# One pool of eight PSUM banks, the last batch's outputs in halves, and a new written order for a fused attention and gated-convolution kernel

## The chip, the cores and the metric

The kernel runs on one core of a Trainium2 chip. A core has TensorE (PE), which multiplies matrices and writes only to PSUM; VectorE (DVE) and ScalarE (ACT), which both read and write PSUM and on-chip memory; GpSimd (POOL); and SyncE (SP), which in this kernel only issues DMA transfers. The engines run side by side, each works through its own instructions in the order in which they are written, and semaphores make one wait for another. PEld in the profile is TensorE's weight load, which overlaps its matmuls.

The metric is the device time of one execution in microseconds (us). Three runs of the kernel before gave 364.24, 364.77 and 365.52 us, a median of 364.77 us.

## The reference

Eight batches `b`, eight heads, 512 tokens, 32 state tokens, head width 64. First each batch goes through a two-way attention between its tokens `x` and its state tokens; both results lie one behind the other, so that a batch then has 544 rows of 512 values. Those rows go through a gated layer of width 1024 with a three-tap convolution along the rows:

```python
scores = scale * x @ state.T            # softmax over 32 state tokens, then @ state   -> xread
scores2 = scale * state @ x.T           # softmax over 512 tokens,      then @ x       -> sread
x = concatenate([xread, sread], axis=2) # heads side by side: (8, 544, 512)
h = maximum(x @ w_in, 0)                # 512 -> 1024
conv = conv_w[0]*h[s-1] + conv_w[1]*h[s] + conv_w[2]*h[s+1]
out = (h * sigmoid(conv)) @ w_out       # 1024 -> 512
```

## The kernel before, in words

**Tiling.** The width of 1024 is cut into eight slices `f` of 128; a step `i = 8 b + f` is one slice of one batch, 64 steps in all. The 512 tokens of a batch are four chunks `c` of 128 rows. The heads are handled in two groups `g` of four.

**One step.** For a batch other than the first, TensorE does six matmuls of 128x128 by 128x512 into a bank `ps_h` (`hidden`, L593): attention weights `a` and the state-times-w_in matrix `u` are each split in a high and a low part of a 32-bit type that TensorE takes in one pass (fp32r), and three of the four products are kept. ScalarE or VectorE takes the bank out as `h` (`relu`, L194 or L196); `middle` (L188 or L190), two taps on VectorE (L619, L624), tanh (L628), `gate` (L633) and a split in high and low (L199, L202) follow. Then `project` (L651) does three matmuls for each of the four chunks into four banks `acc`, which are open over the eight steps of a batch. When they are full, `end` takes each out (L665 on ScalarE, L667 on VectorE) and `store` (L685) sends it off from SP. The first batch goes without the split, in plain fp32 (L588 and L659).

**Beside the steps** stand, for each batch, the scores (`scores`, L300), the transposes of the state tokens' softmax (`flip`, L328), the read of `x` with them (`read`, L341, which needs the transfer `xx`), a small transpose (`read_flip`, L352), and the products of state and w_in (`state_product`, L508, two for each batch but the first; `block_product`, L527, for the first). For the state tokens of four batches at a time there are `state_hidden` (L574) and `tail` (the `acc_t` rows of L651); `tail_store` (L722) sends a lot's rows off in four DMAs. The weights come in through a rounding on ScalarE and VectorE (L237 to L254). In the profile's shapes "128*128", "64*32" and "128*32" say what part of TensorE's array a matmul uses: L651, L593, L588, L574, L328 and L352 use 128*128, L300, L508 and L527 64*32, L341 and L461 128*32.

**Buffers.** PSUM has eight banks. Before, three pools share them: four `acc` (also the first batch's scores and flips), two `ph` (hidden products and the filler), two `ps` (everything else). The transfers `xt` have four buffers, `xx` has one, so that a batch's `xx` can be loaded only when the `read` of the one before is done.

**Order.** Nothing is scheduled when the kernel is built. All work is added as numbered operations with what they read and write, and a written table of these numbers, `ORDER`, says in which order they are issued; a `v` behind a number puts an operation on VectorE that else is on ScalarE, and a negative number puts that many idle matmuls (L209) on TensorE. The words such as "act" or "keep2" that `add` takes, and `IN_TURN`, are not read when the kernel is built. The order of the transfers on SP comes from the same table.

```python
            i = int(word.rstrip("v"))
            if i < 0:
                fns += [self.fill] * -i
                continue
            assert after[i] <= done and i not in done, "an operation before one that it needs"
            fns.append(partial(self.ops[i][2], on=self.vector) if word[-1] == "v" else self.ops[i][2])
```

Of the kernel before, what the change touches and what calls it, by code (L numbers as in the profile page):

```python
# [16 lines left out]
B, H, S, NS, D = 8, 8, 512, 32, 64  # L17
# [10 lines left out]
NL = 4  # L28
# [21 lines left out]
PSUM = dict(acc=4, ph=2, ps=2)  # L50
# [4 lines left out]
121 120 0 98 -10 123 100 99 101 102 103 124v 2 -6 141 4 3 126 5 14 125 -3 149 8 142 15 143 6 17 127 16 7 144 9 -1 444  # L55
# [3 lines left out]
527v 245 455 454 199 495 53 76 512 507 528 513 515v 526 502 514 508 75 516 77 517 160 161 162 52 54 496 550 62 551 201  # L59
# [7 lines left out]
1632 365 366 628 573 602 629 643 615 616 630 119 1633 574 603 617v 632 1634 220 367 644 645 646 587 618 588 647 1635  # L67
# [3 lines left out]
677 693 726 624 328 407 678 679 694 653 332 664 408 234 680 707v 681 665 666 641 656 676 640 237 695 238 696 657 756  # L71
235 333 682 409 708 335 655 757 758 691 709 683 236 741 639 261 593 595 323 654 727 710 667 668 728 730 760 697 410
291 330 670 685 771 414 711 415 712 336 759 729 706 772 773 775 731 331v 337 334 329 405 338 742 743 774 416 411 262
672 669 263 713 776 368 761 684 417 671 745 418 686 698 264 412 699 816 762 413v 374 339 763 764 340 732 765 341 419
420 421 687 714 265 422 718 266 766 746 423 701 777 747 376 700 702 377 369 733 375 267 778 734 717 301 371 372 292
735 748 779 786 715 720 1496 780 719 817v 818 364 721 311 312 787 1497 314 286 736 749 820v 716 315 831 750 801 788
744 781 802v 370 724 313 751 737 268 832 287 833 378 379 722 380 834 269 803 819 804 302 790v 791 789 740 738 270 755
723 271 273 739 792 274 272 835 805 754 282 752 793 794 821 806 836 837 795 767 796 822 753 769 294 770 381 884 382
807 885 886 838 839 303 768 854 869 887 823 808 783 785 855 809 288 784 840 856 824 293 857 304 899 782 810 888 295
799 797 800 275 1498 825 305 858v 900 859 811 889 841 890 815 901 306 860 903 904 870v 278 902 279 871 873 812 798 814  # L80
905 906 1499 289 826 290 1500 861 907 908 276 862 813 827 307 296 1501 297 277 842 829 844 929 828 843 830 1502 845
872 1504 874 308 875 1505 1506 891 424 930 944 1507 914 309 298 1508 892 1509 1510 876 931 425 1512 945 426 846 299
300 863 915 310 909 916 917 847 959 933 1513 864 478 479 918v 484 1514 427 485 1515 482 483 848 934 480 935 849 725
# [3 lines left out]
385 1536 984 1029 1013 1014 1016v 1537 1538 911 913 997 1535 924 966 1539 1540 1541 1017 986 1542 967 895 910 1543 486  # L87
# [3 lines left out]
1007 974 352 1042 346 1043v 979 1020 975 1044 1021 353 1045 995 1059 1030 1072 996 994 1060 1009 1011 1046 1061 355  # L91
347 348 1033 1087 391 1062 356 1022 1034 1088 1063 1047 1035 980 1010 1026 1024 1036 1025 1073 993 1008 1023 1048 1037
349 1064 1039 1038 1040 1049 1074 1075 1089 1091 354 350 1076v 351 1041 393 1092 1050 1093 1051 1052 1077 1155 394
1156 395 1065 1090 1110 1054 1157 1094 1140 1055 396 1078 1079 1111 1066 1080 1159v 1160 1125 1095 1096 1081 1141 1126
1562 1067 1158 1112 1127 1053 1113 1056 1071 397 1082 1068 357 1083 1069 1070 360 358 1128 1142 1097 1161 1129v 1114
1084 361 359 1115 1162 1170 1163 1116 1144 1086 1171 1098 1130 1117 1131 1145 1118 1132 981 1099 1104 1164 1215 1085
1133 392 1134 1119 1146 1216v 1165 1147 1200 1100 1201v 1105 1101 1202 1217 1102 1103 1219 1253 1218 1172 1185 1120
1108 1174 1143 1220 1135 432 1221 1109 1148 1204 1205 1563 1106 1149 1206 1150 1175 1207 1186 1121 1208 1203 1136 1122
1123 1107 1124 1137 439 1152 1167 440 1138 1139 1222 1153 1187 1189v 1254v 1255 1256 1188 1190 1173 1191 1192 1257v
1209 1223 1176 1258 1177 1238 1193 1151 1268 1154 1239v 442 441 1178 1259 1283 1194 1179 1169 1269v 1284 443 1240 1270  # L100
1180 1168 1285 1183 1286 1184 398 1272 1195 399 401 1287v 1210 1288 1166 1289 402 1199 1182 1198 1197 1224 1181 1260
1242 1290 1273 400 1243 1274 1244 1196 1291 1275 1261 1211 1343 1213 1214 1328 1225 1245 1246 1226 1212 1276 1227 1232
1344v 1262 1229 1329v 1241 1330 1313 1247 1298 1263 1332 1248 1299 1333 1251 1345 1300 1228 1271 1301 434 1233 1292
1346 1234 1236 1235 1250 1252 1267 433 1334 1335 437 1302v 1293 1303 1277 435 1331 1314 1315 438 1317 1278 1347v 1230
1231 1237 436 1265 1266 1280 1366 1249 1304 1305 1306 1307 1367 1264 1368 1282 1396 1336 1318 1319 1320 1370v 1279
1348 1294 1371 1349 1337 1281 1297 1295 1372 1426 1338 1308 1397 1350 1310 1351 1321 1322 1381 1398 1373 1369 1316
1400v 1564 1565 1296 1401 1323 1566 1567 1427 1568 1570 1402 1571 1374 1428 1399 1430v 1431 1382v 1383 1311 1326 1384
1572 1385v 1386 1312 1341 1309 1411 1325 1375 1324 1340 1327 1342 1387 1573 1352 1403 1404 1412 1432 1353 1413 1569
1356 1415v 1574 1388 1471 1414 1575 1576 1416 1433 1577 1578 1417 1355 1441 1579 1580 1581 1360 1418 1376 1361 1339
1357 1389 1582 1472v 1473 1583 1474 1584 1475v 1362 1390 1442 1443 1363 1354 1380 1476 1391 1378 1429 1586 1405 1587  # L110
1406 1588 1393 1408 1395 1456 1585 1410 1589 1358 1434 1419 1590 1591 1445v 1446 1592 1594 1595 1457 1359 1364 1596
# [45 lines left out]
def fused_kernel(ctx: ExitStack, tc: tile.TileContext, xT, xn, stT, w_in, conv_w, w_out, out):  # L157
# [49 lines left out]
    def fill():  # L207
        idle.append(bank("idle", "ph")) if not idle else None
        PE.matmul(idle[0][:, :P], ident, ident, start=True, stop=True)  # L209
# [684 lines left out]
```

## Time and profile before

| what | us |
|---|---|
| median of three runs | 364.77 |
| the profiled execution: its time | 364.56 |
| the profiled execution: its span, first to last instruction | 362.8 |
| busy in the span: PE / PEld / DVE / ACT / POOL | 356.2 / 264.7 / 325.0 / 244.8 / 58.8 |

The page's busy times are shares of the span. A matmul's row runs from its start to the modelled end of its pipeline, so that rows of neighbours overlap, and a TensorE that reads as busy may still wait between two starts. The chain of waits, which follows the last instruction back through what released it, shows the net piece of each group of matmuls instead; from such pieces one sees how long a group holds TensorE. VectorE's and ScalarE's rows overlap by a little too. Times in a view are in us from the start of the span unless marked ns, and "x24" says how many instructions a row groups. Transfers run on 16 DMA engines; the windows' last two columns give their busy share and the GB/s moved.

### The profile page before, as it was taken

To read this page: it belongs to the slowest core of one execution; us is meant where nothing else is said; L and a number is where in the kernel's file an instruction comes from. 1 tells how busy PE (TensorE), PEld (TensorE's weight loads), DVE (VectorE), ACT (ScalarE), POOL (GpSimd) and SP (SyncE) were. 2 spreads that over 40 slices of the span, in tenths; PEclk is the share of its full clock that TensorE was granted. 3 is DMA by queue.
4 is the path that set the end of the run, shared out by engine and by line. 5 is a ranking of instruction groups with operands and counts; after the bars stand their busy time and mean duration, and the time that the engine had idled before them with its cause. 6 is when DMAs were issued, how large, how long until landed. Compare 5 with 4: busy or idle time off the path is not lost.

```text
span 362.8 us, 6645 instructions
## 1 busy us (share of the span) xinstructions
PE 356.2 (98%) x2498; PEld 264.7 (73%) x2498; DVE 325.0 (90%) x577; ACT 244.8 (67%) x494; POOL 58.8 (16%) x159
## 2 busy tenths in 40 slices
PE   7999999999999999999999999999999999999995
PEld 6753557676668876878898877877877778888884
DVE  2999999999999999999999999988989968988761
ACT  2999998885868777565857665845764457445731
POOL 1014103130201112130101201111312212111000
PEclk9999999999999999999999999999999999999999
DMA  7999784033240342200020012000200002002004
GB/s 247 399 357 394 285 327 142 2 117 116 78 157 0 117 146 75 101 4 0 31 87 0 2 58 89 30 0 3 82 33 2 0 29 89 1 0 89 30 2 144
DMA packets 12384, 35.05 MB, mean 97 GB/s; under 512 B 1472, under 2 KB 2880, under 8 KB 11328
## 3 DMA queue, kind: packets, MB, share of 16 engines
q1 hardware_dynamic: 12352, 34.63, 26.2%
q8 instruction: 19, 0.31, 0.3%
q14 instruction: 13, 0.11, 0.1%
HBM read 25.71 MB, written 8.91 MB: 95 GB/s over the span
## 4 chain that ended last, share of the span: by engine, by line
PE 89%; ACT 4%; DVE 3%; DMA 1%; issue 1%; SPq 0%; DVEq 0%
PE acc L651 45%; PE ps_h L593 21%; PE ps_u L508 4%; PE ps_h L588 4%; PE acc_t L651 3%; PE ps_s L300 2%; PE ps_hs L574 2%; PE acc_c L651 2%; PE ps_r L341 1%; DMA st<-stT 1%; PE ps_t L328 1%; PE ps_s L461 1%; PE idle L209 1%; ACT e L319 1%; ACT hc L237 1%
## 5 line engine op out<-in xcount | busy, mean ns | idle before, releaser
L651 PE MATMUL acc<-wo,g 128*128 128x512 f32 x708 | 175.8, 394 | 0.1
L651 PEld LDWEIGHTS acc<-wo,g 128*128 128x128 f32 x708 | 130.8, 188 | 36.8 <-issue 5.0
L593 PE MATMUL ps_h<-a,u 128*128 128x512 f32 x336 | 84.9, 393 | 0.0
L593 PEld LDWEIGHTS ps_h<-a,u 128*128 128x128 f32 x336 | 62.3, 188 | 18.0 <-issue 2.5
L199 ACT ACTIVATE g<-t 128x512 fp32r<-128x512 f32 (+1 forms) x60 | 36.9, 621 | 21.2 <-DVE t L633 14.0
L619 DVE SCALAR_TENSOR_TENSOR t<-h,cw,t 128x511 f32<-128x511 f32 x64 | 47.4, 746 | 1.8 <-ACT t L188 1.5
L608 POOL COPY hs<-h 128x1 f32<-128x1 f32 x64 | 27.0, 436 | 132.5 <-ACT h L194 109.9
L624 DVE SCALAR_TENSOR_TENSOR t<-h,cw,t 128x512 f32<-128x512 f32 (+1 forms) x64 | 47.1, 745 | 1.4
L603 POOL COPY h<-hs 128x1 f32<-128x1 f32 x56 | 25.3, 458 | 136.0 <-DVE t L633 127.9
L628 ACT ACTIVATE t<-t 128x512 f32<-128x512 f32 x64 | 39.6, 627 | 11.0 <-DVE t L624 10.7
L202 DVE TENSOR_TENSOR g<-t,g 128x512 fp32r<-128x512 f32 (+1 forms) x60 | 40.2, 676 | 3.7 <-ACT g L199 3.4
L633 DVE SCALAR_TENSOR_TENSOR t<-t,h 128x512 f32<-128x512 f32 (+1 forms) x64 | 41.8, 663 | 1.6 <-ACT t L628 1.4
L194 ACT ACTIVATE h<-ps_h 128x512 f32<-128x512 f32 x51 | 30.1, 595 | 14.1 <-PE ps_h L593 11.1
L188 ACT ACTIVATE t<-h,cw 128x512 f32<-128x512 f32 x40 | 28.3, 720 | 1.3 <-DVE h L196 1.0
L665 ACT ACTIVATE o<-acc 128x512 f32<-128x512 f32 (+1 forms) x30 | 17.3, 584 | 12.9 <-PE acc L651 12.6
L199 ACT ACTIVATE u<-ps_u 128x512 fp32r<-128x512 f32 x28 | 16.1, 595 | 10.4 <-PE ps_u L508 10.4
L202 DVE TENSOR_TENSOR u<-ps_u,u 128x512 fp32r<-128x512 f32 x28 | 18.7, 681 | 2.8 <-ACT u L199 2.8
L574 PEld LDWEIGHTS ps_hs<-sr,wi 128*128 128x128 f32 x128 | 14.9, 192 | 1.1 <-ACT sr L356 0.4
L508 PE MATMUL ps_u<-wi,st 64*32 64x512 f32 x224 | 15.2, 601 | 0.0
L588 PE MATMUL ps_h<-p,u 128*128 128x512 f32 x32 | 15.2, 608 | 0.0
L574 PE MATMUL ps_hs<-sr,wi 128*128 128x128 f32 x128 | 15.2, 276 | 0.0
L240 ACT ACTIVATE raw<-raw 128x512 uint32<-128x512 uint32 (+1 forms) x17 | 11.2, 669 | 5.8 <-DMA raw<-conv_w 4.8
(95 smaller groups left out, 409.9 us busy)
## 6 DMA issues: line engine op xcount, KB each, us to landing
xt<-xT SPq DMA_DIRECT2D x16, 512.0 KB, 6.3
xx<-xn SPq DMA_DIRECT2D x8, 1024.0 KB, 5.1
out<-o SPq DMA_DIRECT2D x30, 256.0 KB, 2.1
raw<-w_in SPq DMA_DIRECT2D x8, 512.0 KB, 6.9
raw<-w_out SPq DMA_DIRECT2D x8, 512.0 KB, 9.0
out<-o_t SPq DMA_DIRECT2D x8, 64.0 KB, 1.7
st<-stT SPq DMA_DIRECT2D x1, 448.0 KB, 5.5
out<-o_c SPq DMA_DIRECT2D x1, 256.0 KB, 2.8
```

What stands on the lines that cost most here:

```text
L194: A.activation(dst, src, AF.Relu, scale=0.5)
L199: A.activation(hi, src, AF.Copy)
L202: engine.tensor_tensor(lo, src, hi.bitcast(F32), op=ALU.subtract)
L508: PE.matmul(ps_u[b, hf, g][j * NS:(j + 1) * NS, :], st[half, b * NP + j, :], wi[half, j, hf * 512:(hf + 1) * 512], start=True, stop=True)
L574: PE.matmul(ps_hs[m, f][:, :NT], wi[:, k, f * P:(f + 1) * P], sr[m][:, k, :], start=(k == 0), stop=(k == NK - 1))
L588: PE.matmul(ps_h[i], u[0][:, g, fs], pa[0][:, g, :], start=(g == 0), stop=(g == NG - 1))
L593: PE.matmul(ps_h[i], u[j][:, g, fs], a[k][:, g, :], start=(n == 0), stop=(n == 3 * NG - 1))
L619: V.scalar_tensor_tensor(t[:, 1:], h[:, :S - 1], cw[:, f, 0:1], t[:, 1:], op0=ALU.mult, op1=ALU.add)
L624: V.scalar_tensor_tensor(t[:, :n], h[:, 1:n + 1], cw[:, f, 2:3], t[:, :n], op0=ALU.mult, op1=ALU.add)
L628: A.activation(tt[i], tt[i], AF.Tanh, scale=0.25)
L633: V.scalar_tensor_tensor(tt[i][:, :n], tt[i][:, :n], 1.0, hd[i][:, :n], op0=ALU.add, op1=ALU.mult)
L651: PE.matmul(acc, g[j][:, cs], wo[:, k, f, :], start=(f == 0 and n == 0), stop=(f == NF - 1 and n == 2))
```

## The change

Five things are different.

1. **One pool.** The pools `acc=4`, `ph=2`, `ps=2` become one pool `ps=8`. Every bank is asked for from it, so that an `acc`, a hidden product or a transpose may take any free bank, and the tags by which operations wait for each other become ("ps", ...).
2. **The last batch's outputs.** Batch 7 was stored in whole chunks of 128x512, only its last chunk in two halves of 128x256; now all four chunks are evacuated and stored in halves. Their buffers come from `xt`, `xt`, `e2` and `o`. An `end` can now be put on ScalarE or on VectorE by the table.
3. **Stores of state tokens.** The four DMAs of a lot's state tokens were one operation; each is now an operation that the table can place by itself.
4. **The table.** `ORDER` is written anew as a whole: the numbers of later operations are shifted by the added ones, the filler goes from 23 matmuls to 18, and the v-marks are others. By the built order 9 `middle`, 3 `relu` and the 2 `e2t` copies go from VectorE to ScalarE, one copy of `u` goes the other way, and six of the output evacuations are on VectorE (3 whole, 3 halves), before two. Beyond the filler, no matmul is added or dropped.
5. **Names of kinds** (`mid2`, `vk2`, `store1`), which the built kernel doesn't read.

```diff
-PSUM = dict(acc=4, ph=2, ps=2)
+PSUM = dict(ps=8)
...
 ORDER = """
-121 120 0 98 -10 123 100 99 101 102 103 124v 2 -6 141 4 3 126 5 14 125 -3 149 8 142 15 143 6 17 127 16 7 144 9 -1 444
...
-1491
+120 121 0 98 -10 123 99 100 101 102 8 103 9 124v -6 141 2 11 10 125 3 149 126 142 12 -1 143 150 151 13 127 14 4 15 131
...
+1497 1488 1486 1487 1489 1470 1485 1498 1500 1499 1501
...
-            ps_s[NG * b + g] = bank(f"ps_s_{b}_{g}", "ps" if b else "acc")
+            ps_s[NG * b + g] = bank(f"ps_s_{b}_{g}")
...
-        ps_h[i] = bank(f"ps_h_{i}", "ph")
+        ps_h[i] = bank(f"ps_h_{i}")
...
-            accs[b, c] = bank(f"acc_{b}_{c}", "acc")
+            accs[b, c] = bank(f"acc_{b}_{c}")
...
     def parts_of(b, c):
-        n = 2 if (b, c) == (B - 1, NCH - 1) else 1
+        n = 2 if b == B - 1 else 1
...
-    def out_tag(b, c):
-        return "o" if b < B - 1 else "xt" if c < NCH - 1 else "e2"
-
-    def end(b, c, q, engine):
+    def out_tag(b, c, q):
+        return "o" if b < B - 1 else ("xt", "xt", "e2", "o")[c]
+
+    def end(b, c, q, on=A):
...
-    def tail_store(m):
-        o = outs["t", m]
-        for i in range(NL):
-            nc.sync.dma_start(out[NL * m + i, S:, :], o[i * NS:(i + 1) * NS, :])
+    def tail_store(m, i):
+        nc.sync.dma_start(out[NL * m + i, S:, :], outs["t", m][i * NS:(i + 1) * NS, :])
...
-                    on = b == B - 1 and (c + q) % 2
-                    cost = ("tt3" if on else "keep2") if parts > 1 else "tt" if on else "act"
-                    o = (out_tag(b, c), "o", b, c, q)
-                    add("DVE" if on else "ACT", cost, partial(end, b, c, q, V if on else A),
-                        r=[("acc", b, c)], w=[o])
+                    o = (out_tag(b, c, q), "o", b, c, q)
+                    add("ACT", "keep2" if parts > 1 else "act", partial(end, b, c, q), r=[("ps", "acc", b, c)], w=[o],
+                        other="vk2" if parts > 1 else "tt")
...
-            add("SP", "store", partial(tail_store, m), r=[("o", "t", m)])
+            for i in range(NL):
+                add("SP", "store1", partial(tail_store, m, i), r=[("o", "t", m)])
```

What the new table moves, at the three places of which the prediction speaks. In these rows the name left of the arrow is the tile written, those right of it are read, and the last number of a name counts buffers.

TensorE, in the middle of the program, before: the product of state and w_in of batch 4 (`ps_u`, eight matmuls of 32x512) stands alone between a hidden product or projections of full width.

```order
L593 MATMUL ps_h_1768<-a_2_1363,u_2_1_1409 128x512
L651 MATMUL acc_1_1339<-wo,g_15_1540 128x512
L651 MATMUL acc_1_1339<-wo,g_15_1539 128x512 x2
L508 MATMUL ps_u_0_0_1794<-wi,st 32x512
L508 MATMUL ps_u_0_1_1795<-wi,st 32x512
...
L651 MATMUL acc_2_1314<-wo,g_15_1540 128x512
L651 MATMUL acc_2_1314<-wo,g_15_1539 128x512 x2
```

The change, the same product: the read of `xx` of another batch (`ps_r`, 32 matmuls) now stands directly ahead of it.

```order
L651 MATMUL acc_1_1374<-wo,g_14_1609 128x512
L651 MATMUL acc_1_1374<-wo,g_14_1608 128x512 x2
L341 MATMUL ps_r_1679<-xx_1638,e2t_1673 32x64 x16
L341 MATMUL ps_r_1679<-xx_1638,e2t_1629 32x64 x16
L508 MATMUL ps_u_0_0_1716<-wi,st 32x512
L508 MATMUL ps_u_0_1_1717<-wi,st 32x512
...
L651 MATMUL acc_3_1344<-wo,g_14_1609 128x512
L651 MATMUL acc_3_1344<-wo,g_14_1608 128x512 x2
```

Before, TensorE left the full-width matmuls twice for these two pieces of work; now it leaves them once.

SP, the first transfers, before: the `xx` of the first batch stands behind the seventh block of weights (`raw`).

```order
L233 DMA raw_257<-w_in 128x2x512
L233 DMA raw_319<-w_in 128x1024
L233 DMA raw_326<-w_in 128x1024
L233 DMA raw_335<-w_in 128x1024
L292 DMA xx_373<-xn 128x2048
L233 DMA raw_420<-w_in 128x1024
L836 DMA st<-stT 128x896
```

The change: the rest of the state (`st`), five `xt` and six weights stand ahead of it.

```order
L233 DMA raw_241<-w_in 128x2x512
L833 DMA st<-stT 128x896
...
L288 DMA xt_433<-xT 128x1024
L288 DMA xt_435<-xT 128x1024
L233 DMA raw_439<-w_out 128x1024
L288 DMA xt_493<-xT 128x1024
L292 DMA xx_495<-xn 128x2048
```

The `xx` of the first batch went from the twelfth transfer of the program to the twenty-first.

SP, the last stores, before: the four stores of state tokens stand between the last two stores of outputs.

```order
L685 DMA out<-o_3_1_3945 128x256
L685 DMA out<-o_3_0_3958 128x256
L685 DMA out<-o_0_0_3953 128x512
L685 DMA out<-o_1_0_3955 128x512
L722 DMA out<-o_t_3975 32x512 x4
L685 DMA out<-o_2_0_3987 128x512
```

The change: they stand ahead of the eight halves of the last batch, and the last store is a half.

```order
L720 DMA out<-o_t_3936 32x512 x4
L685 DMA out<-o_2_0_3955 128x256
L685 DMA out<-o_1_1_3969 128x256
...
L685 DMA out<-o_0_1_3976 128x256
L685 DMA out<-o_3_0_3988 128x256
L685 DMA out<-o_3_1_3990 128x256
```

Between the last store of state tokens and the program's last store stand seven halves now; before nothing stood between them.

More of the change, by code (lines that the diff above doesn't have):

```diff
@@ L71 @@
[L71 to L80, printed above, removed]
@@ L92 @@
[L92 to L101, printed above, removed]
@@ L102 @@
[L102 to L106, printed above, removed]
@@ new lines @@
+144 -1 145 20 5 17 129 6 21 22 132 146 147 16 23 7 444 18 447 148 1 44 32 46 33 240 239 24 19 152 134 153 25 130 135
+45 445 154 35 47 48 450 451 446v 26 155 448 34 449 156 38 27 242 49 29 28 30 243 245 128 31 40 452 39 244 41 36 42 37
[13 rows of a table added]
+625 664 640 690 228 238 678 661 665 652 235 666 236 627 692v 706 334 676 667 642 233 286 653 668 337 368 404 403 406
[4 rows of a table added]
+765 314 816 421 751 370 315 779 263 372 808 377 788 287 340 715 831 832 264 766 790v 833 809 774 265 737 791 266 722
+292 724 341 817 780 818 378 375 820v 792 267 270 740 271 819 755 804 789 273 793 835 725 268 723 289 752 738 753 770
@@ new lines @@
+272 739 290 294 754 295 769 794 269 720 781 274 784 869 422 301 854 767 302 721 288 810 870 379 768 783 782 899 282
+834 380 795 871 873 855 884 856 836 821 303 1503 822 796 823 304 858v 874 857 824 305 825 811 423 885 886 1504 837 296
[9 rows of a table added]
+973 1013 1548 1014 1550 1016 1043 974 985 975 1044 390 1541 1551 988 1087 1046 976v 1003 1552 989 1553 1004 342 1554
+980 981 1047 1017 990 1005 1018 1555 991 957 992 1556 1006 972 1072 1549 1019 1073 1020 1015 1074 1048 1021 1057 1558
+1058 393 352 1559 343 1022 978 1007 1560 344 486 1036 487 1076 1088 996 1557 1561 1077 1049 1562 1050 391 1037 979
@@ new lines @@
+1563 355 345 993 1059 1089 1045 1060 1090 1011 1026 1008 1023 995 1041 1564 356 346 994 1010 1091v 347 353 348 394
+1051 1025 1078 349 1052 350 1009 1038 1024 1565 1039 354 1040 351 1054 1055 395 1140 1566 1061 1079 1080 396 397 1092
+1062 1567 1063 1064 1141 392 1155 1569 977 1093 1065 1570 1156v 1571 1094 1053 1110 1125 1066 1142 1075 1568 1143 1095
+1067 1126 1081 1157 1144 1111v 1112 1127 1129 1082 1145 1146 1130 1238 1056 357 1069 1159 358 1128 1070 1147 1084 1085
+1071 360 1114v 1148 1131 1115 1283 1068 359 361 1116 1117 1132 1096 1133 1097 1160 1185 1083 1186 1086 1200 1100 1149
@@ new lines @@
+1101 1161 1170 1158 1187 1188 1113 1098 1150 1201 1162 1134 1215 1099 1163 1189 1118 1190 1135 1119 1106 1108v 1120
+1171v 1124 1216 1109 1107 1164 1172 1174v 1122 1104 1175 1165 1137 398 1139 1105 432 1123 1176 1177 401 399 1178 1102
+1103 1202 1173 1217 402 1204v 1219 1138 1205 1220 1218 1239v 1206 1153 1152 1121 1136 1168 1151 1240 1166 1268 400
+1191 1242 1241 1298 1253 1179 1180 1192 1193 1243 1221 1194 1222 1195 1244 1223 1245 1299 1246 1269v 1154 1169 1184
+1199 1183 1270 1271 1167 1207 1272v 433 1208 1209 1181 1196 434 1210 1254 1273 1255 1203 1300 1224 1284 1285 1256 1286
@@ new lines @@
+1225 1572 1257v 1182 1197 1343 1212 1274 1258 1287 435 437 1275 1211 1227 438 436 1276 1247 1248 1302v 1313 1214 1198
+1314 1232 1213 1303 1228 1288 1328 1315 1289 1290 1291 1304 1259 1260 1234 1235 1277 1366 1261 1344v 1278 1317 1305
+1262 1233 1329v 1345 1301 1346 1330 1306 1263 1318 1251 1332 1229 439 1226 1333 440 1250 442 1367 1292 443 1249 1266
+1265 1252 1267 1293 1264 1279 1280 1319 1334 1335 1347 1320 1336 1368 1370v 1282 1369 1371 1316 1348 1573 1281 1294
+1381 1574 1307 1236 1321 1372 1575 1349 1373 1322 1230 1382v 1576 1396 1297 441 1374 1577 1441 1411 1350 1397v 1308
@@ new lines @@
+1337 1579 1295 1296 1398 1351 1442 1399 1331 1383 1443 1426 1323 1400v 1445v 1471 1311 1326 1310 1401 1338 1309 1312
+1385 1402 1327 1580 1578 1386 1403 1444 1324 1384 1581 1342 1404 1582 1583 1231 1237 1352 1584 1585 1325 1387 1388
+1587 1472v 1389 1588 1412 1589 1353 1413 1473 1590 1591 1592 1446 1427 1428 1447 1430 1448 1390 1340 1355 1341 1456
+1586 1474 1414 1593 1431 1595 1357 1596 1597 1391 1598 1375 1376 1599 1449 1378 1339 1600 1601 1429 1415 1475 1457
+1458 1416 1417 1432 1611 1364 1418 1405 1379 1356 1594 1612 1602 1380 1394 1354 1365 1476 1406 1613 1614 1459 1460v
@@ L207, in fill @@
     def fill():
-        idle.append(bank("idle", "ph")) if not idle else None
+        idle.append(bank("idle")) if not idle else None
         PE.matmul(idle[0][:, :P], ident, ident, start=True, stop=True)
@@ L364, in attention @@
         add("PE", "scores", partial(scores, b), r=[("st", int(b > 0)), ("xt", NG * b), ("xt", NG * b + 1)],
-            w=[("at", b)] + [("ps", "s", b, g) if b else ("acc", "s", g) for g in range(NG)])
+            w=[("at", b)] + [("ps", "s", b, g) if b else ("ps", "acc", "s", g) for g in range(NG)])
         for g in range(NG):
-            add("ACT", "act", partial(keep_scores, NG * b + g), r=[("ps", "s", b, g) if b else ("acc", "s", g)] + [("at", b)] * g,
+            add("ACT", "act", partial(keep_scores, NG * b + g), r=[("ps", "s", b, g) if b else ("ps", "acc", "s", g)] + [("at", b)] * g,
                 w=[("scores", b, g)] if g else [("at", b), ("scores", b, g)], other="tt")
@@ L448, in first_flip @@
     def first_flip(g):
-        ps_x[g] = bank(f"ps_x_{g}", "acc")
+        ps_x[g] = bank(f"ps_x_{g}")
         for c in range(NCH):
@@ L487, in first_softmax @@
     def first_softmax(g):
-        x, s, m, n, p = ("acc", "x", g), ("acc", "s", g), ("s1", "m0", g), ("s1", "s0", g), ("pa", g)
+        x, s, m, n, p = ("ps", "acc", "x", g), ("ps", "acc", "s", g), ("s1", "m0", g), ("s1", "s0", g), ("pa", g)
         add("PE", "flip", partial(first_flip, g), r=[("scores", 0, g), ("at", 0)], w=[x])
@@ L779, in step @@
             r += [(x, b, f // 4, q) for x in ("uhi", "ulo") for q in range(NG)]
-        add("PE", "hidden" if b else "hidden0", partial(hidden, i), r=r, w=[("ph", i)])
-        add("ACT", "act", partial(relu, i), r=[("ph", i)], w=[h], other="tt")
+        add("PE", "hidden" if b else "hidden0", partial(hidden, i), r=r, w=[("ps", "h", i)])
+        add("ACT", "act", partial(relu, i), r=[("ps", "h", i)], w=[h], other="tt")
         if b:
@@ L784, in step @@
         add("POOL", "pool", partial(edge, i), r=[h], w=[("edge", i)] + ([("corner", f)] if b == 0 else []))
-        add("ACT", "middle", partial(middle, i), r=[h, ("weight", W_CONV)], w=[t], other="two")
+        add("ACT", "middle", partial(middle, i), r=[h, ("weight", W_CONV)], w=[t], other="mid2")
         add("DVE", "tap", partial(before, i), r=[h], w=[t])
@@ L799, in step @@
                 r=[*g, ("weight", W_OUT + f) if i >= WHOLE else (f"g{f % 2}", "w", f)],
-                w=[("acc", b, c)])
+                w=[("ps", "acc", b, c)])
         if f == NF - 1:
```

20 lines of the change are left out of this document (6 added, 14 removed), and 49 rows, old and new, of the table ORDER.

## The prediction

> **What bounds the kernel now.** I read four views: the page's busy shares, the windows, the groups of TensorE by shape, and the chain of waits in order of time. The busy shares first, and four windows of the first half (columns: engine busy us with instruction counts for PE, PEld, DVE, ACT, POOL; granted clock; DMA share; GB/s).
>
> ```profile
> span 362.8 us, 6645 instructions
> ...
> PE 356.2 (98%) x2498; PEld 264.7 (73%) x2498; DVE 325.0 (90%) x577; ACT 244.8 (67%) x494; POOL 58.8 (16%) x159
> ```
>
> ```profile
> 0.00:10.00 10.00, 7.89 (x56) 6.79 (x57) 2.78 (x8) 3.48 (x7) 1.73 (x23) 1.00 0.81 260
> 10.00:20.00 10.00, 9.94 (x193) 7.60 (x195) 9.50 (x23) 9.42 (x22) 0.00 (x0) 1.00 1.01 389
> 20.00:30.00 10.00, 10.00 (x140) 4.33 (x132) 9.93 (x20) 8.80 (x18) 3.42 (x3) 1.00 1.01 371
> 30.00:40.00 10.00, 10.00 (x60) 3.68 (x53) 9.96 (x19) 9.77 (x20) 2.47 (x8) 1.00 1.01 401
> ...
> 100.00:150.00 50.00, 50.00 (x454) 37.09 (x453) 49.00 (x84) 38.10 (x79) 7.31 (x20) 1.00 0.30 107
> ```
>
> Two candidates stand out, TensorE with 98% and VectorE, which is full from 10 to 150 us (9.96 of 10, 49.00 of 50). A matmul's busy row overlaps its neighbour's, so 98% proves nothing. What decides is whether TensorE's own pieces fill the time. The chain gives the piece that a group really holds:
>
> ```profile
> 75.61 1.02 PE ps_s L300 x16
> 76.63 2.96 PE ps_h L593 x12
> ...
> 98.39 5.44 PE acc L651 x24
> ...
> 112.45 0.44 PE ps_t L328 x4
> ...
> 141.10 1.03 PE ps_r L341 x64
> 142.13 1.58 PE acc L651 x6
> ```
>
> ```profile
> 205.97 0.89 PE ps_hs L574 x8
> 206.86 2.06 PE acc L651 x9
> ...
> 214.36 1.02 PE ps_u L508 x16
> 215.38 5.00 PE acc L651 x21
> ```
>
> A full-width fp32r matmul (L651, L593) costs 5.44/24 = 0.227 us. Behind a narrow group (L300, L341, L508, shapes 64*32 and 128*32) it costs more: 12 should take 2.72 and take 2.96, 6 should take 1.36 and take 1.58, 21 should take 4.76 and take 5.00. So each visit to a narrow shape costs 0.22 to 0.24 us beside its own work. Behind L574, whose shape is 128*128, nine take 2.06 where 2.04 is due: such a visit costs about 0.03.
>
> The groups from 69.6 us on say what TensorE has to do there.
>
> ```profile
> L651 PE MATMUL acc<-wo,g 128*128 128x512 f32 x699 | 172.9, 393 | 0.1
> L593 PE MATMUL ps_h<-a,u 128*128 128x512 f32 x336 | 84.9, 393 | 0.0
> L508 PE MATMUL ps_u<-wi,st 64*32 64x512 f32 x208 | 14.2, 601 | 0.0
> L651 PE MATMUL acc_t<-wo,gts 128*128 128x512 f32 x48 | 13.4, 391 | 0.0
> L574 PE MATMUL ps_hs<-sr,wi 128*128 128x128 f32 x72 | 8.5, 275 | 0.0
> L651 PE MATMUL acc_c<-wo,last 128*128 128x512 f32 x24 | 5.7, 391 | 0.0
> L328 PE MATMUL ps_t<-ident,e 128*128 128x128 f32 x32 | 4.8, 272 | 0.0
> L341 PE MATMUL ps_r<-xx,e2t 128*32 128x64 f32 x256 | 4.4, 220 | 0.0
> L300 PE MATMUL ps_s<-xt,st 64*32 64x512 f32 x48 | 3.3, 601 | 0.0
> ```
>
> 1107 fp32r matmuls at 0.227 are 251.0; 13 L508 products of 1.02 are 13.3; 9 pieces of L574 at 0.89 are 8.0; 32 flips at 0.11 (the piece of four L328 is 0.44) 3.5; 4 reads at 1.03 and 3 scores at 1.02 make 7.2. Together 283.0 of the 288.9 us from 69.6 to the end of the last matmul at 358.5. Of the missing 5.9, the order has 20 narrow visits there (20 x 0.24 = 4.8) and some 14 wide ones (0.4). Only 0.7 us is left. **TensorE is the bound and hardly ever starves after 70 us**; VectorE runs full beside it and just keeps up. So a gain must come from three places: the front, the visits, and the tail behind the last matmul.
>
> **The visits.** The tally by the built orders, from the first fp32r product on: before, 22 narrow visits, each entered from and left to full width, 44 seams between shapes. In the change the products of state and w_in are put behind a read, beside scores or beside L574, as the order rows ahead show: 12 narrow visits, 24 seams, and 4 inside them where L341 meets L508 or L300. That is 28, 16 fewer, at half of 0.24 each: 1.9 us. Against it, visits to wide fp32 shapes grow from 15 to 21, since L574 now comes in small pieces: 6 x 0.03 = 0.2. Sum: -1.7. No row shows a seam between two narrow shapes. If those four are free it is 20 x 0.12 - 0.2 = -2.2; if all ten joints inside joined visits cost like a seam, those with L574 and those between equal shapes too, it is -1.0. I take the middle, since the shapes of L341 and L508 differ as those of L508 and L651 do.
>
> The Trainium skill, TensorEngine Tiling (Array Packing), Key Properties, says that a change of the tiling mode drains TensorE, and a change of the tile alone does not. The trace agrees for entering and leaving (0.22 to 0.24 us); by that rule L341 behind L508 is no free neighbour and the term is the -1.7, where joints at no cost would give -2.2.
>
> **The pool** adds no instruction. It allows the joints, which need three banks at once. Its price would be a wait for a bank that ScalarE or VectorE has not emptied; TensorE would then starve, and the built order puts every first projection behind at least as much other TensorE work as before (15.0 us after its hidden product, 12.9 before, by the same prices). I take zero.
>
> **The copies.** Net 13 scalings and relus go from VectorE to ScalarE, and VectorE gets four more evacuations. ScalarE's mean in the window from 100 to 150 is 38.10/79 = 0.48, so 13 are some 6 us over the whole program. TensorE hides it: ScalarE has 12 of 50 us free there. In the front, where it has none (9.77 of 10), it would count in full, but ahead of the first fp32r product stand 100 ScalarE and 110 VectorE operations now, against 103 and 113. Zero. The five dropped idle matmuls stood in waits: zero.
>
> **The front.** From the chain, and from the views of SP and of the tile `xx`:
>
> ```profile
> 20.87 0.89 PE ps_r L341 x64
> 21.76 3.63 PE ps_h L588 x8
> 25.39 1.95 PE ps_s L300 x16
> ```
>
> ```profile
> 28.76 0.60 SPq L292 DMA_DIRECT2D xx<-xn x1
> ```
>
> ```profile
> DMA to landing us min/median/max: 4.8/5.1/10.9
> ```
>
> The first hidden product starts at 21.76. In the change the scores of batch 3 (1.02) stand ahead of it in the place of the first read (0.89), and VectorE has 25 instead of 27 operations ahead of the reciprocal that opens the last spread. I take 21.8 again. Then before loses 1.95 - 1.02 = 0.93 us on an `xt` that has not landed. In the change the first read stands 12 rows of L588 (5.45), scores, a block product (1.02 each) and 8 rows of L588 (3.63) later, at 32.9, with three seams 33.2. Its `xx` is now the 21st transfer and, with its own bytes, 10.5 MB deep (from the shapes). The windows move 2.6 + 3.9 + 3.7 = 10.2 MB by 30 us and 0.40 a us then, so its last byte moves at 30.8. How much later it lands I take from the second `xx` of before: 13.1 MB deep, moved at 37.2, issued at 28.76 and landed 10.9 later at 39.7, so 2.5. It lands at 33.3: a wait of 0.1 to 0.3. The second `xx` is 13.7 MB deep and lands at 41.2; the read comes 7.5 us of TensorE's work after the first, at 41.0. Two waits of about 0.3 take the place of 0.93: -0.3. Bounds: no wait at all, -0.9; four reads each 0.6 late, +1.5.
>
> **The tail.**
>
> ```profile
> 357.14 1.37 PE acc L651 x6
> ...
> 358.53 0.60 ACT o L665
> ```
>
> ```profile
> 357.80 1.73 SPq L722 DMA_DIRECT2D out<-o_t x4
> 359.63 0.37 SPq L685 DMA_DIRECT2D out<-o x1
> ```
>
> ```profile
> out<-o SPq DMA_DIRECT2D x30, 256.0 KB, 2.1
> ...
> out<-o SPq DMA_DIRECT2D x2, 128.0 KB, 1.7
> ```
>
> ```profile
> L665 ACT ACTIVATE o<-acc 128x256 f32<-128x256 f32 x1 | 0.4, 384 | 0.2 <-PE acc L651 0.2
> ```
>
> Last matmul done at 358.51, evacuated at 359.13, but SP is with the four small stores until 359.53: the last store goes at 359.63 and lands 2.1 later, 3.2 after the last matmul. In the change 27 fp32r matmuls (6.1 us) follow the last of `acc_t`, so the four stores are gone before. Two halves of 0.38 follow each other on ScalarE; SP issues the first 0.45 after the last matmul and the second about 0.9 after, landing at 2.6. Gain 0.6; if SP, with twelve issues of some 0.43 in the last six us, is one behind, 0.2. I take -0.45.
>
> **Sum.** 362.8 - 0.3 - 1.7 - 0.45 = 360.35 us of span; the execution's own 364.56 becomes 362.1, and on the median of the runs, 0.2 higher, **362.3**.
>
> **The rivals.**
> - *The front eats the gain.* ScalarE (9.77 of 10) or the `xx` waits cost 1.5 to 2 us more than before. For it: 33.2 against 33.3 is no margin, nor is 41.0 against 41.2. Against it: every load of the change is needed no earlier, in bytes ahead, than the rows allow. 364.77 + 1.5 - 2.15 = 364.1.
> - *Slower: the chain of the one `xx` buffer.* A load may go only when the read before is done and takes 4.8 alone, 10.9 in a full queue. If the first lands late, each next one starts late. It decides when the four reads wait 4.2 us in all, about 1.05 each, so from a first landing at 34.3 on. With 1.1 each: 4 x 1.1 - 0.93 - 2.15 = +1.3, 366.1. For it: the first `xx` went back nine places. Against it: between reads lie 7.5 us of TensorE's work.
> - *The seams are not the shapes'.* If the 0.24 is a price of each piece of work, joined or not, only front and tail remain: 364.77 - 0.75 = 364.0. Against it: L574 shows nearly none.
> - *VectorE is the bound.* Then what it loses counts: net nine operations at 49.00/84 = 0.58 are 5.2 us, 364.77 - 5.2 - 0.45 = 359.1. For it: 49.00 of 50. Against it: the sum of TensorE's pieces, which leaves 0.7 us for any starving. The Trainium skill, Perfetto Trace Analysis, Identifying the Most-Contended Engine, says to judge TensorE by its weight loads' share instead of its matmuls'; that share is 73%, under VectorE's 90%, and leads to this rival. The pieces disagree.
> - That the change doesn't do what it says is excluded for the order, which is built as the rows show.
>
> **How the numbers follow.** About 0.3% (1.1 us) is what this measurement tells from no change. Forecast 0.66 (its own range 361.1 to 363.7, mostly); front eats the gain 0.14; seams 0.08; slower 0.07; VectorE 0.05. Faster takes the forecast, VectorE and 0.02 of the first rival, 0.73; same 0.20; slower 0.07. The range of 361.0 to 364.6 takes in the two rivals at 364 and leaves out the slower one and VectorE's.
>
> **What would show it.** Right: in the chain of the change a read followed by an L508 piece without extra between, then one 0.22 to 0.24 behind; 5.9 us missing becoming some 4.2; pieces of L300 at 25 to 28 us at 1.02; the last store issued 0.9 us behind the last matmul. Wrong: `ps_r` pieces well above 1.03 ahead of 60 us with `xx` as releaser; a gap of issue or of SP's loads in the chain between 21 and 45 us of more than the 0.93 us that before has there; issue or ACT pieces in the chain after 70 us.

## The result

Over eight executions each, the change took a median of 362.24 us (360.42 to 364.57) and the kernel before 365.53 us (364.24 to 366.79). The ratio is 0.9906, with a 95% interval of 0.9879 to 0.9933: faster by 0.9%. The prediction was 362.3 us, in a range of 361.0 to 364.6, from a sum that gave -2.45 us of span. The profiled execution took 361.51 us with a span of 359.7, so 3.1 us less than the 362.8 of before. The total is right; its terms are not: the front came out worse than forecast, the visits and the tail better. Executions more than 1.5% above the fastest of their version are left out of the medians and ratios below.

From the page of the change, the span and the busy shares, which look as before and decide nothing:

```profile
span 359.7 us, 6635 instructions
...
PE 351.5 (98%) x2488; PEld 266.0 (74%) x2488; DVE 319.6 (89%) x568; ACT 248.0 (69%) x506; POOL 67.6 (19%) x159
```

**The front.** TensorE's rows in order of time (start, duration, group) give the first fp32r product; first the kernel before, then the change.

```profile
63.06 0.95 PE L651 MATMUL acc<-wo,g 128*128 128x512 f32 x3
```

```profile
63.29 0.95 PE L651 MATMUL acc<-wo,g 128*128 128x512 f32 x3
```

The work that TensorE has ahead of this row shrank by 1.6 us: five idle matmuls less (1.1; each has two records of 0.11, as in the row `9.81 0.67 PE idle L209 x6` of the chain before) and, by the prices of the prediction, 0.5 of pieces that now stand behind it. Yet it comes 0.23 later. So TensorE lost 1.8 us more ahead of it, or 0.7 net of the idle matmuls. The chain of the change says where (start, duration, what; L237 and L470 are on ScalarE, L237 takes the magnitude of a weight block):

```profile
7.86 9.78 DMA raw<-w_in
...
17.71 0.67 ACT hc L237
18.39 0.49 ACT p L470
...
18.92 1.05 PE ps_x L474 x8
19.98 0.93 PE ps_u L527 x16
20.91 1.86 PE ps_s L461 x32
22.77 1.38 PE ps_s L300 x16
24.15 5.35 PE ps_h L588 x12
```

The second exponential of the first attention (L470) waits behind a weight block that lands at 17.63, since L237 stands ahead of it in ScalarE's queue. The waits of TensorE between 15 and 64 us (waited us in total, times, longest) are these; before, the same view lists none:

```profile
PE ps_t L328 <- DVE p L485: 1.3, 1, 1.3
PE ps_x L474 <- ACT p L470: 0.8, 1, 0.8
PE ps_r L341 <- DMA xx<-xn: 0.3, 1, 0.3
```

L328 is the second flip, L474 the sum over the second group's exponentials, and L485 a division on VectorE that empties a PSUM bank.

The windows show what followed (PE, PEld, DVE, ACT, POOL busy with counts, granted clock, DMA share, GB/s):

```profile
16.00:18.00 2.00, 0.73 (x20) 0.42 (x4) 1.96 (x4) 0.85 (x3) 0.00 (x0) 1.00 1.01 410
18.00:20.00 2.00, 1.19 (x17) 1.06 (x24) 1.14 (x2) 2.00 (x5) 0.00 (x0) 1.00 1.04 418
20.00:22.00 2.00, 2.00 (x40) 1.17 (x44) 1.92 (x6) 1.62 (x6) 0.00 (x0) 0.52 0.99 375
22.00:23.00 1.00, 1.00 (x24) 0.52 (x24) 0.18 (x2) 1.00 (x4) 0.00 (x0) 0.50 1.08 291
```

TensorE is busy 1.92 of 4 us, and then its granted clock is half of full. In that stretch the 32 spreads L461 take 1.86 us in the chain and the scores L300 1.38, where 1.02 is due. Before, the same spreads took 1.01:

```profile
19.86 1.01 PE ps_s L461 x32
```

**The visits.** The chain of the change, two joined visits:

```profile
126.53 2.77 PE acc L651 x12
129.30 1.03 PE ps_r L341 x64
130.33 1.02 PE ps_u L508 x16
131.35 1.59 PE acc L651 x6
```

```profile
96.95 1.02 PE ps_s L300 x16
97.97 0.86 PE ps_u L508 x16
```

L508 behind L341 takes its own 1.02, and the six full-width matmuls behind it 1.59, where 1.36 is due: 0.23, once for both pieces. Where the two shapes are the same (L300, L508), the second takes 0.86 instead of 1.02 besides. Behind its first fp32r product, TensorE has 289.4 us of own work, by the prices of the prediction, up to the last matmul at 356.21, 292.9 us in all; before, it had 288.9 of 295.4. What is not own work fell from 6.6 to 3.5 us.

**The tail.** The chain ends with the last matmuls, and SP's rows show the last stores:

```profile
350.08 6.13 PE acc L651 x27
```

```profile
350.79 1.74 SPq L720 DMA_DIRECT2D out<-o_t  x4
352.63 4.82 SPq L685 DMA_DIRECT2D out<-o  x8
```

```profile
out<-o SPq DMA_DIRECT2D x8, 128.0 KB, 1.8
```

The last matmul ends at 356.21, SP's last store ends its issue at 357.45, and the span ends 3.5 us behind the last matmul; before, 4.3.

**The balance**, from the prices of single pieces:

| term | predicted | measured |
|---|---|---|
| front: waits and clock, less the idle matmuls dropped | -0.3 | +1.8 - 1.1 = +0.7 |
| visits, from the first fp32r product on | -1.7 | -3.0 |
| tail | -0.45 | -0.75 |
| span | -2.45 | -3.05 |

### The profile page after: what moved, and what is told of

Its sections match the earlier page's. It is cut to its first block, busy times and chain, and to the rows that moved or that the text cites. A ratio compares the mean times of both kernels' runs of the same rounds, so it can differ in the third digit from the quotient of the medians.

```text
span 359.7 us, 6635 instructions
## 1 busy us (share of the span) xinstructions
PE 351.5 (98%) x2488; PEld 266.0 (74%) x2488; DVE 319.6 (89%) x568; ACT 248.0 (69%) x506; POOL 67.6 (19%) x159
## 4 chain that ended last, share of the span: by engine, by line
PE 92%; DMA 6%; SPq 0%; ACT 0%; issue 0%; DVE 0%; ACTq 0%; DVEq 0%
PE acc L651 45%; PE ps_h L593 21%; PE ps_hs L574 4%; PE ps_h L588 4%; PE ps_u L508 4%; PE acc_t L651 3%; DMA raw<-w_in 3%; PE ps_r L341 2%; DMA xx<-xn 2%; PE ps_s L300 2%; PE acc_c L651 2%; PE ps_t L328 1%; PE acc L659 1%; DMA raw<-conv_w 1%; PE ps_s L461 1%; PE ps_u L527 0%
## 5 line engine op out<-in xcount | busy, mean ns | idle before, releaser
L651 PE MATMUL acc<-wo,g 128*128 128x512 f32 x708 | 173.7, 393 | 0.0
L593 PE MATMUL ps_h<-a,u 128*128 128x512 f32 x336 | 83.9, 391 | 0.0
L603 POOL COPY h<-hs 128x1 f32<-128x1 f32 x56 | 32.4, 588 | 166.4 <-DVE t L633 138.2
L608 POOL COPY hs<-h 128x1 f32<-128x1 f32 x64 | 29.2, 475 | 95.6 <-ACT h L194 87.2
L194 ACT ACTIVATE h<-ps_h 128x512 f32<-128x512 f32 x54 | 32.4, 599 | 19.4 <-PE ps_h L593 12.7
L188 ACT ACTIVATE t<-h,cw 128x512 f32<-128x512 f32 x49 | 34.8, 724 | 4.2 <-DVE g L202 2.3
L665 ACT ACTIVATE o<-acc 128x512 f32<-128x512 f32 (+1 forms) x29 | 15.8, 554 | 6.8 <-PE acc L651 4.9
L574 PEld LDWEIGHTS ps_hs<-sr,wi 128*128 128x128 f32 x128 | 16.6, 191 | 3.2 <-ACT t L188 0.8
L574 PE MATMUL ps_hs<-sr,wi 128*128 128x128 f32 x128 | 17.0, 276 | 0.0
L237 ACT ACTIVATE hc<-raw 128x512 f32<-128x512 f32 (+1 forms) x17 | 11.3, 666 | 7.6 <-DMA raw<-conv_w 4.4
L588 PE MATMUL ps_h<-p,u 128*128 128x512 f32 x32 | 14.8, 599 | 0.0
L508 PE MATMUL ps_u<-wi,st 64*32 64x512 f32 x224 | 14.8, 598 | 0.0
```

The source lines that it names most:

```text
L188: A.activation(dst, src, AF.Copy, scale=scale)
L194: A.activation(dst, src, AF.Relu, scale=0.5)
L574: PE.matmul(ps_hs[m, f][:, :NT], wi[:, k, f * P:(f + 1) * P], sr[m][:, k, :], start=(k == 0), stop=(k == NK - 1))
L593: PE.matmul(ps_h[i], u[j][:, g, fs], a[k][:, g, :], start=(n == 0), stop=(n == 3 * NG - 1))
L603: G.tensor_copy(hd[i][:, S:], hs[m, f][:, j, 1:2])
L651: PE.matmul(acc, g[j][:, cs], wo[:, k, f, :], start=(f == 0 and n == 0), stop=(f == NF - 1 and n == 2))
```

## The experiments

Numbers in the table of the order are operations; 152 is the second exponential L470, 134 the second flip L328, 130 and 135 the copies of both flips (L188), 153 the second sum L474, 46 and 33 a rounding (L240) and a magnitude (L237) of weights. All ran beside the kernel before. The runs on the idle matmuls and on the exponential shared one chip; those on the pool, the joints, ScalarE's queue and the whole chunks a second; those on the loads of `xx`, with the repeat of the change, a third.

### One pool alone

```diff
 def bank(name, tag="ps"):
-    return psum.tile([P, 512], F32, tag=tag, name=name, bufs=PSUM[tag])
+    return psum.tile([P, 512], F32, tag="ps", name=name, bufs=8)
```

> The kernel before with all its banks from one pool of eight; order, transfers and everything else as before. Theory (the pool by itself does nothing, it only allows the joints): 365.5 as before, first L588 and first fp32r product within 0.3 us of before. Rival (banks that wait for one another's readers across kinds cost time in the front, or more freedom gains some): off by over 1 us, seen as waits of TensorE for ScalarE or VectorE ahead of L328, L527 or L588.

365.84 us against 365.45, ratio 1.0008 (0.9992 to 1.0024). The first L588 starts at 21.96, the first fp32r product at 64.00, 0.9 later than in the one trace of before. That is more than the 0.3 that the theory allowed and less than the 1 us that the rival asked for; the times show nothing of it. In time the pool alone is worth nothing either way.

### The joints taken apart

One projection is moved between the two halves of seven joined visits, as here for a read (419, batch 7) and a state product (311, batch 4); 700 is the projection ahead of them:

```diff
-700 419 764 748 311
+419 764 748 700 311
```

> In the change one projection of three full-width matmuls is moved between the two halves of each of seven joined visits: L300 or L508 behind L508 or L300 (three, equal shapes) and L341 with L508 or L300 (four, unequal shapes). Nothing is added or dropped. Theory (a visit away from the full-width matmuls costs 0.22 to 0.24 us, however many narrow shapes it holds; joints are free): 7 x 0.24 = 1.7 us more time of TensorE behind its own work from 69.5 us on (3.4 becomes 5.1), and a little more where equal shapes overlapped; median 363.9 to 364.4. The prediction's middle (a joint between unequal shapes costs a seam of 0.12): 3 x 0.24 + 4 x 0.12 = 1.2. Rival (the price is one of each piece of work): no change, 3.4 and 362.2.

364.32 us, 0.9979 of before (0.9954 to 1.0003): what is left of the gain over before is within the noise. The chain at the place shown above:

```profile
127.79 2.08 PE acc L651 x9
129.87 1.03 PE ps_r L341 x64
130.90 0.89 PE acc L651 x3
131.79 1.02 PE ps_u L508 x16
132.81 1.58 PE acc L651 x6
```

Three full-width matmuls between the halves take 0.89 where 0.68 is due, and six behind take 1.58: two visits of 0.21 and 0.22, where one of 0.23 stood. From 69.5 us on TensorE loses 5.3 us beside its own work instead of 3.4: +1.9 for seven joints, 0.28 each. The prediction's middle said 1.2, the price per visit 1.7 "and a little more where equal shapes overlapped". The four unequal joints make 4 x 0.21 and the three equal ones 3 x (0.21 + 0.16), together 1.95. No wait of TensorE is listed behind 64 us, and the other engines have the same operations as in the change. So the seams are the shapes', a joint costs nothing whether its shapes are equal or not, and a price of each piece of work, joined or not, is out.

### The idle matmuls

Put back into the change, where TensorE waited:

```diff
-152 134 153
+152 -5 134 -3 153
```

```diff
-                fns += [self.fill] * -i
+                fns += [partial(self.fill, n == 0 and len(done) > 30) for n in range(-i)]
...
-    def fill():
-        idle.append(bank("idle")) if not idle else None
+    def fill(new=False):
+        idle[:] = [bank("idle")] if new or not idle else idle
```

> Eight idle matmuls are put into the change, five ahead of the second flip (L328) and three ahead of the second sum (L474), where TensorE waited 1.27 and 0.81 us between 16.2 and 18.9 us; nothing else differs. Theory (the idle matmuls that the change dropped kept TensorE's granted clock up): the granted clock no longer falls to half between 20 and 24 us, the 32 spreads L461 take 1.01 instead of 1.86 and the scores L300 1.02 instead of 1.38, the first L588 starts 1.2 us earlier, near 22.9 us, the mean clock of every run is 0.999 or more, and the median is 360.4 to 360.9. Rival (the low clock comes and goes by itself, and the spread of the change's times has another cause): clocks of 0.991 to 1.0 as before and 362.2. Second rival (the idle matmuls themselves delay what follows): first L588 at 24 or later.

362.84 us (0.9945, 0.9923 to 0.9967), not better than the change, and the executions' mean clocks ran from 0.990 to 1.0 again. Each of the two groups asks for a bank of its own. In the profiled one the clock stayed at 1.00 and L461 and L300 took 1.04 and 1.02, as expected; but the first L588 still started at 23.69. The chain tells why:

```profile
17.97 0.48 ACT p L470
18.45 0.49 ACT e2t L188
18.94 0.04 issue
18.99 0.66 PE ps_t L328 x4
19.64 0.67 PE idle L209 x6
20.32 0.79 PE ps_x L474 x8
```

The flip now got a bank only when ScalarE had copied the other flip out (`e2t`, L188), which also stands behind the late weight, and the idle matmuls took 0.67 behind that. The low clock goes with some 1.2 us in the rows L461 and L300 of the change's profiled execution (0.85 + 0.36), but it is not what makes the first L588 late.

The other way round, five idle matmuls taken from the kernel before (`-3`, `-1`, `-1` in the table):

> The kernel before without five of its idle matmuls (the three ahead of the second flip L451 and the two single ones ahead of the sum and of the block product of the second group); nothing else differs. Theory (idle matmuls hold the clock): the granted clock falls in the first 25 us in some or all runs, mean 0.99 to 0.997, and those runs are 1 to 3 us longer, median 366 to 368. Rival (they only stand in waits and do nothing, as the prediction costed them): clock 0.999, 365.5.

365.12 us against 365.78, ratio 0.9988 (0.9971 to 1.0006), clocks of 0.997 to 1.0, first fp32r product at 62.53 instead of 63.06. The rival holds, and more: there, idle matmuls that went away harmed nothing. So these runs give no sign that costing them at nothing was an error.

### The exponential alone, and both

```diff
-44 32 46 33 240 239 24 19 152 134 153
+44 32 152 46 33 240 239 24 19 153 134
```

> In the change the exponential of the first batch's second group (L470) is put ahead of one rounding and one absolute value of weights (L240, L237) on ScalarE, so that it no longer stands behind a weight that landed at 17.63 us; the second flip (L328) goes behind the sum (L474) that needs it. Theory (the first hidden product is late because this exponential waits in ScalarE's queue behind a late weight): L470 ends near 16.5 instead of 18.88, the first L588 starts at 22.0 to 22.8 instead of 24.15, and with a shorter idle time the clock mostly stays up; 360.5 to 361.2. Rival (the chain of the spread is bound by VectorE or by the state's product anyway): first L588 at 23.8 or later and no gain, 362.2.

363.02 us (0.9924, 0.9906 to 0.9942): no gain over the change. The first L588 starts at 24.52. TensorE's waits:

```profile
PE ps_r L341 <- DMA xx<-xn: 1.7, 2, 1.1
PE ps_t L328 <- ACT e2t L188: 1.7, 1, 1.7
```

The exponential was not the only operation behind the late weight: the copies of the flips (L188) are there too, and the second flip waits for the bank that the first copy frees.

The same, with five idle matmuls ahead of 153 (`-5` in the table), which ask for a bank of their own, by the same edit of `fill` as above:

> The early exponential together with five idle matmuls ahead of the sum (L474). Theory: both terms add where they don't overlap; clock 0.999 or more in every run, first L588 at 21.5 to 22.3, median 359.5 to 360.4. If the clock was the whole loss, the same as with the idle matmuls alone; if the queue was, the same as with the early exponential alone.

366.0 us (0.9979, 0.9949 to 1.0009), with executions from 362.4 to 367.6; the first L588 at 24.02 in the profiled one. The theory failed. In that execution the clock stays at 1.00, but the idle matmuls themselves wait 1.6 us for the bank that the first copy L188 frees, as the second flip did without them. Why this version is 3 us worse than either of its parts is not settled: its profiled execution is one of its shortest.

### ScalarE's queue

```diff
-132 146 147 16 23 7 444 18 447 148 1 44 32 46 33 240 239 24 19 152 134 153 25 130 135
+132 146 147 134 16 23 7 444 18 447 148 1 44 32 152 130 135 46 33 240 239 24 19 153 25
```

> In the change three ScalarE operations of the first attention (the second exponential L470 and the two copies of the flips L188) are put ahead of a rounding (L240) and an absolute value (L237) of weights, whose block landed at 17.2 to 18.0 us in the change, with idle matmuls and with the early exponential; the second flip (L328) goes ahead of the first block products, where a bank is free. Theory A (the front's loss is ScalarE's queue: work for the attention stands behind a late weight, and the idle TensorE then gets half the clock): no wait of TensorE above 0.5 us between 15.5 and 20 us, clock at 1.00 from 20 to 24 us, first L588 at 21.0 to 22.3 instead of 24.08, clocks of 0.998 or more in all runs, median 359.5 to 360.8. Theory B (the weights are late in the transfers, and whatever needs them waits, so that the place of the wait moves only): first L588 earlier, but the first fp32r product again at 63 or later, median 362 to 363. Theory C (the low clock comes by itself): clocks spread from 0.99 to 1.0 as in the change.

361.73 us (0.9899, 0.9878 to 0.9919), all executions between 361.29 and 362.77. Theory A holds for its part: the first L588 starts at 22.03, no waits ahead of it above 0.2, clock 1.00. But the first fp32r product comes at 63.43, as late as in the change, as theory B said, and the median lies between the ranges of the two theories. The mean clock was 0.995 in two of the six executions, below the 0.998 that theory A asked for in all. The waits now:

```profile
PE ps_r L341 <- DMA xx<-xn: 1.9, 2, 1.1
```

Two microseconds won at the first L588 are lost again before two reads of `xx`.

### The loads of xx

In addition, the first `xx` (122) goes ahead of a w_out load (56), and two `xt` (280 and 322) behind the third `xx` (159):

```diff
-50 ... 198 199 490 56 ... 157 122
+50 ... 198 199 490 122 56 ... 157
...
-280 ... 322 159
+159 322 280
```

> The reordered ScalarE queue of act_front and, on SP, the first xx two places earlier (ahead of the second w_out load) and two xt loads (for batches 4 and 5) moved behind the third xx. In act_front the first L588 started 2.05 us earlier than in the change, but the reads L341 then waited 0.9 and 1.1 us for xx, and the first fp32r product came at 63.43, as late as in the change (63.29). Theory (the front has two bounds of nearly equal length, ScalarE's queue and the transfers of xx through one buffer; only both together give anything): reads wait less than 0.3 us, first fp32r product at 61.2 to 62.0, median 359.3 to 360.6. Rival (the DMA engines are full, so an earlier xx only makes other loads late): new waits ahead of scores L300 or weights, first fp32r product at 63 or later, 361.7 or more.

360.36 us against 365.46, ratio 0.9855 (0.983 to 0.9879): it beats the kernel before clearly; beside the change its interval just touches that of the change on the same chip (0.9874 to 0.9943, below). In the chain all four reads take their own 1.03 and none waits, and the first fp32r product stands 1.5 us earlier than in the change:

```profile
33.87 1.03 PE ps_r L341 x64
...
41.23 1.03 PE ps_r L341 x64
...
49.57 1.03 PE ps_r L341 x64
...
57.10 1.03 PE ps_r L341 x64
```

```profile
61.78 0.93 PE L651 MATMUL acc<-wo,g 128*128 128x512 f32 x3
```

The clocks of its executions were 0.998 to 1.0.

The moves on SP alone, with ScalarE's queue as in the change:

> The change with the moves on SP alone (first xx two places earlier, two xt loads behind the third xx), ScalarE's queue as in the change. Theory of two bounds: in the change the reads wait only 0.3 us, so nothing is to be had: first L588 near 24, first fp32r product at 62.8 to 63.5, median 361.8 to 362.8. Rival (transfers alone bind): first fp32r product at 62 or earlier and a median of 361 or less.

362.68 us (0.9916, 0.9886 to 0.9947): as the theory of two bounds says for the time. Its profiled execution, at 363.07 one of the middle ones, has its first fp32r product at 64.84, later than expected. Two reads wait 2.0 us for `xx` there, so the moves on SP don't remove that wait by themselves.

The change itself, on the same chip:

> The change itself on the same chip as the two others, to compare them with it without the difference of chips, and to see how far its front varies from one execution to the next: 361.8 to 363, clocks of 0.99 to 1.0; the longer an execution, the lower its mean clock, since both come from a TensorE that waits in the front.

362.25 us against the same 365.46, ratio 0.9908 (0.9874 to 0.9943). In both series of the change, executions at a clock of 0.999 or 1.0 took 360.4 to 361.1, at 0.995 361.5 to 362.5, at 0.990 or 0.991 363.3 to 364.6. So the time of the change goes with the clock of its front, which varies. Two other versions left that front as it is, and their profiled executions show how far: with the joints apart the first fp32r product stands at 63.60 and a read waits 1.4 us for `xx`, with whole chunks (below) 66.76 and 1.1. The version with both repairs gains 1.9 us on the median and 1.3 on the best execution (359.07 against 360.41), so most of its gain is there in the best execution too and some 0.6 is steadiness; with five executions each, that split is rough.

### The last batch's chunks whole again

```diff
-        n = 2 if b == B - 1 else 1
+        n = 2 if (b, c) == (B - 1, NCH - 1) else 1
```

> The change with chunks 0 to 2 of the last batch evacuated and stored whole, as before; the last chunk stays in halves and last, and the stores of state tokens stay ahead. Theory (the tail's gain comes from the order: the last store is a half, and nothing stands ahead of it on SP): from the last matmul to the end of the span 3.4 to 3.6 us as in the change, median 362.2. Rival (the halves of the other chunks carry it): 3.9 to 4.2 us, median 362.7.

363.60 us (0.9947, 0.9925 to 0.9968); its front was late in the profiled execution (first L588 at 26.28), so the tail is read from the trace alone. The last matmuls and SP's last stores:

```profile
353.54 6.13 PE acc L651 x27
```

```profile
356.09 4.82 SPq L685 DMA_DIRECT2D out<-o  x5
```

The span of 363.4 ends 3.7 us behind the last matmul at 359.67, 3.5 in the change and 4.3 before. That lies between what the theory (3.4 to 3.6) and the rival (3.9 to 4.2) asked for: in this trace, halving the other chunks gives 0.2 of the tail's gain and the order the other 0.55.

## Why the prediction was right, and where it was not

**The total** came out right because the front's miss of +1.0 makes up for most of the misses of the visits (-1.3) and the tail (-0.3). That the median meets the forecast to 0.1 us is luck besides: the forecast started from 364.77, the median of three runs, and eight gave 365.53, so that the gain is 3.3 us where 2.5 was forecast. None of the rivals holds as a whole.

**What bounds the kernel**: right. Behind the first fp32r product, no wait of TensorE is listed in the change, and what it loses beside its own work is the visits. VectorE as the bound is out: it lost nine operations, its windows stayed full (49.11 of 50 from 100 to 150 us), the gain sits where the visits are, and parting the joints took 2 us back with VectorE's operations unchanged.

**The visits**: the mechanism is right, the term was sized wrongly. Two steps failed. "I take the middle", a seam of 0.12 between L341 and L508: it measured nothing, so the end of -2.2 was the better reading. And pieces of equal shape were taken at 1.02 each, joined or not; the second, or the first, takes 0.86 when its neighbour has its shape. Part of what a lone L508 is charged with is thus already the price of leaving it. Some 0.3 of the -3.0 is not accounted for by either. The rule that the prediction quoted from the Trainium skill, TensorEngine Tiling (Array Packing), Key Properties, that a change of the tiling mode drains TensorE, agrees for the way from and to the full width (0.21 to 0.23 us here); between L341 and L508, whose shapes differ too, no run here shows such a price.

**The front**: the step that failed is the start of the first hidden product, "I take 21.8 again". It counted VectorE's operations ahead of the last spread (25 against 27) and not what stands ahead of L470 and of the two flips' copies on ScalarE, and when the weight that these wait behind lands: 17.63. It started at 24.08; 1.2 of the 2.3 us stand in the two rows at half clock. The count of ScalarE's operations (100 against 103) was right and said nothing, since the order, not the number, changed. That the change moved these operations behind two weights is seen in ScalarE's order, which the prediction did not read at this place.

**The `xx` loads**: right in mechanism, and for the landing in the change's trace also in the number. The estimated landing was 33.3, the issue at 24.59 and 8.7 us to landing give 33.3. Because the front was 2.3 late, it was waited for only once, 0.3 us, in this execution; in two others with the same front the wait was 1.4 and 1.1. With the front repaired, the two waits came as the prediction had them for a start at 21.8, only larger: 1.9 in all instead of 0.6.

**The pool at zero**: right for the time of the pool alone. But in the front there is a wait that the prediction took at zero: the second flip waits 1.3 us for the bank that L485 frees. It is hidden there by the wait of L474, and whether the pool or the new order brings it was not taken apart.

**The tail**: right in mechanism. The last store is issued 0.86 behind the last matmul, as predicted (0.9); a half lands 1.8 behind its issue instead of 2.1 for a whole chunk, and the end of the program behind that took 0.2 less, so that the gain is 0.75.

## What to carry to other kernels

Count the excursions from one matmul shape to another as visits, not as seams: two narrow pieces side by side cost one visit, and here every joint was worth 0.28 us. Where an operation on the critical path shares an in-order queue with work that needs a transfer, what counts is when the transfer of its neighbour ahead lands, not how many operations stand ahead. And in a front with two bounds of nearly equal length (here ScalarE's queue and the loads of one buffer), repairing one moves the wait; of the versions tried, the one with both was the fastest.

## What was not expected of the hardware

The granted clock of TensorE fell to half for some 3.5 us from 20 us on, after a stretch of 4 us in which it was busy for 1.92, its longest wait 1.3 us. The Trainium skill, TensorE: Matmul & The Clock Gate, Part 1: The HAM clock gate, gives about 3.4 us of idle time as what sends the clock to half; here waits that were much shorter, with little work between them, were enough. In the kernel that repaired the front, TensorE was busy 9.20 of the 10 us from 10 to 20, and the clock stayed at 1.00. The busy share alone does not decide. With the joints apart, TensorE was busy for 2.94 of the 4 us from 12 to 16, its longest wait 1.1, and the clock fell to 0.54; with the early exponential and idle matmuls together it was busy for only 2.43 of the 4 us from 16 to 20, its wait 1.6, and the clock stayed (columns as in the windows above):

```profile
12.00:16.00 4.00, 2.94 (x48) 2.34 (x46) 2.82 (x8) 2.88 (x6) 0.00 (x0) 1.00 1.03 393
16.00:18.00 2.00, 1.94 (x41) 1.52 (x47) 1.60 (x4) 1.77 (x4) 0.00 (x0) 0.54 1.02 412
```

```profile
16.00:20.00 4.00, 2.43 (x66) 1.96 (x59) 3.47 (x6) 2.69 (x5) 0.00 (x0) 1.00 1.00 396
20.00:24.00 4.00, 4.00 (x78) 2.40 (x76) 1.95 (x7) 2.49 (x8) 0.00 (x0) 1.00 0.96 311
```

What decides was not measured. Idle matmuls went with a full clock in the profiled executions of both versions that had them put back, but other executions of these versions fell to 0.990 or 0.989.
